# Attention scores as three float32r products of split keys and queries in a fused attention and two-layer MoE kernel

## The chip, the cores and the metric

The program runs on one NeuronCore of a Trainium2 chip. The metric is device time in microseconds (us) of one execution; lower is better. PE is TensorE, DVE is VectorE, ACT is ScalarE, POOL is GpSimd, SP is the engine whose queue issues the transfers.

## What is computed

Inputs are float32: attention with 2 batches, 8 heads, 576 positions and 64 values per head, with a bias on every score that comes out of a small network of the distance of two positions, and then two layers of the form activation(x @ w_in) @ w_out over 1152 tokens.

```python
scores = scale * np.matmul(q, k.transpose(0, 1, 3, 2))
x = (psi_rel / psi_i)[..., None]
bias = np.maximum(x @ w1 + b1, 0.0) @ w2
scores = scores + bias.transpose(2, 0, 1)[None]
attn = softmax(scores)                     # over the last axis
x = np.matmul(attn, v)                     # tokens x 512
h = x @ moe_w_in;   x = (max(h, 0) + alpha * min(h, 0)) @ moe_w_out
h = x @ moe2_w_in;  g = (a0 + a1 h + a2 h^2 + a3 h^3) / (1 + |b0| |h| + |b1| h^2 + 1e-6)
out = g @ moe2_w_out
```

## The kernel before

**Attention.** The queries are cut into nine blocks (BLOCKS): eight of 128 queries of one batch, and a last one with the 64 remaining queries of both batches side by side. Each block has four steps, one for a pair of heads, so there are 36 steps, 0 to 35; steps 32 to 35 are those of the last block. The two heads of a pair lie on partitions 0 to 63 and 64 to 127, of keys and of queries alike.

A step goes through these functions: `scores` (L326) multiplies keys and queries on PE, each head in its own half of the array's rows, 288 columns at a time, both operands float32, which the compiler makes two instructions of each; `row_max` (L338, DVE) adds the bias and takes the row's maximum; `expo` (L349, ACT) exponentiates and sums; `flip` (L361, L365, PE) transposes the result in nine pieces; `flip_out` (L371 and L375 on DVE, L377 on ACT) copies them out of PSUM; `values` (L389, PE) multiplies by the values. There is room in PSUM for the scores of one step only (pool `ps_s`), and the ninth transposed piece of step n goes into a spare corner of the scores of step n+1 where the new order holds, so PE can write scores of a step only after `row_max` has read those of the step before.

After a block's last step `inverse` (L400 to L402, DVE) takes 1/sum, `block_scale` (L442, DVE) applies it, and `block_split` (L450 on ACT, L451 on POOL) writes the result as a high part, rounded to float32r, and the low rest.

**Bias.** Between the steps the bias of the next blocks is made, in rows j, r: `hidden` (L228 on ACT, L230 on DVE), `bias_mm` (L244, PE), `bias_out` (L256 and L263 on ACT, L258 and L265 on DVE), and `bias_move`, a transfer on SP's queue (L270, L274). Row set j = 0 is made before step 0. For j = 4, the last block's 64 queries, the rows are made for partitions 0 to 63 and `bias_again` (L278) copies them to partitions 64 to 127 on DVE, in four pieces after steps 29 to 32.

**MoE.** Weights come in as 64-bit pieces; `unit_scale`, `unit_rest` (L613, L617, ACT) and `unit_join` (L621, L624, DVE) put a float32 together, `unit_high` (L644 on ACT, L646 on DVE) rounds it to float32r and `unit_low` (L651) subtracts for the rest. The first 12 units (`UHS`) have the rounding on DVE and the subtraction on POOL, the others have them on ACT and DVE. All MoE products are three float32r products, high by high, high by low and low by high (`up` L682, `down` L697).

**Order.** Nothing is reordered by the tools. Each call is put on an agenda with a planned time out of the table `Z`, and the agenda, sorted by that time, is the program order on every engine. `step_time(n)` is the planned start of step n. Two orders of a step exist: the older one, where flips and bias products alternate, and a new one for steps `FIRST` to `LAST`, 8 to 35, where the flips of step n-1 follow the scores of step n and the values are multiplied in four column tiles of 32 (`wide`) rather than two of 64.

Of the kernel before, what the change touches and what calls it, by code (L numbers as in the profile page):

```python
# [11 lines left out]
F32 = mybir.dt.float32  # L12
# [38 lines left out]
def row_tables():  # L51
# [54 lines left out]
def fused_kernel(ctx: ExitStack, tc: tile.TileContext, qT, q4T, kT, vp, m1_in, m1_out, m2_in, m2_out, small, ttab, out):  # L106
# [46 lines left out]
    xu_p = open_pool("xu", 1, "left")  # L153
    rq_p = open_pool("rq", 3, "left")
    bb_p = open_pool("bb", 1, "left")
# [19 lines left out]

    KT = [ac.tile([P, 4, S], F32, name=f"kt{b}") for b in range(B)]
    V = [ac.tile([P, 5, H, D], F32, name=f"v{b}") for b in range(B)]
# [17 lines left out]

    queries = {}

    def load_k(b, hp):
        nc.sync.dma_start(out=KT[b][:, hp], in_=kT[b, :, hp])

# [3 lines left out]
    def load_q(k):  # L204
        ib, b = BLOCKS[k]
        t = rq_p.tile([P, 4, P], F32, tag="rq", name="q")
        if ib < 4:
            nc.sync.dma_start(out=t, in_=qT[ib, b])
        else:
            for b in range(B):  # L210
                nc.sync.dma_start(out=t[:, :, 64 * b : 64 * b + 64], in_=q4T[b])
        queries[k] = t

    bias, hid, bev, bps = {}, {}, {}, {}
# [52 lines left out]
    def bias_move(j, r):  # L267
        be, bt = bev.pop((j, r)), bias[j]
        if j < 4:
            nc.sync.dma_start(out=bt[r::8].rearrange("p h j -> p (h j)"), in_=be)  # L270
        else:
            for i in range(2):
                rows = bt[2 * r + i : 64 : 8].rearrange("p h j -> p (h j)")
                nc.sync.dma_start(out=rows, in_=be[64 * i : 64 * i + 64])  # L274

    def bias_again(h):

        nc.vector.tensor_copy(out=bias[4][64:, h : h + 2], in_=bias[4][:64, h : h + 2])  # L278

# [29 lines left out]

    FIRST, LAST = 8, 36  # L310
    ptile, pps, tps, ptt, sums, pvs, spare = {}, {}, {}, {}, {}, {}, {}

    def scores(n):

        k, hp = divmod(n, 4)
        ib, b = BLOCKS[k]
        ptile[n] = p_p.tile([P, 2, S], F32, tag="p", name="p")
        if hp == 0:
            sums[k] = sm_p.tile([P, H], F32, tag="sums", name="sums")
        for u in range(2):  # L320
            pps[n, u] = ps_s.tile([P, 2, 512], F32, tag="s", name="s")
        for w in range(2):
            for bb, cols in [(b, slice(0, P))] if ib < 4 else [(0, slice(0, 64)), (1, slice(64, P))]:
                for u in range(2):
                    rows = slice(64 * u, 64 * u + 64)
                    nc.tensor.matmul(  # L326
                        out=pps[n, u][cols, w, :HALF], lhsT=queries[k][rows, hp, cols],
                        rhs=KT[bb][rows, hp, w * HALF : (w + 1) * HALF], start=True, stop=True,
                    )
        spare[n] = pps[n, 1][:, 1, HALF : HALF + P]  # L330
# [95 lines left out]
    def by_tensor(k):  # L426
        return k >= 6
# [60 lines left out]
    for n in range(NSTEP):  # L488
# [12 lines left out]
        if hp == 3:  # L501
            ag.at(t + Z["inv"], inverse, k)
            scale = t + 3 * DT + Z["new_bscale"] if FIRST <= n + 2 < LAST else t + 3 * DT + Z["bscale"]
            if by_tensor(k):
# [17 lines left out]
    NWA, NWC, NWB, NMID, NSP = 5, 2, 13, 13, 3  # L522
    UHS, USP = 12, 48
    NW = NWA + NWC + NWB
# [47 lines left out]
    def next_pools():  # L572
        for key in ("ba", "bb", "rq"):
            close_pool(key)
# [63 lines left out]
    def unit_high(j):  # L638
# [284 lines left out]
```

## Time and profile before

| | us |
|---|---|
| median of 3 runs | 604.25 (603.94 to 604.37) |
| profiled execution, its own time | 604.18 |
| its span | 602.4 |
| mean granted TensorE clock | 0.997 of full speed |
| PE busy | 586.9 (97%) |
| DVE busy | 500.1 (83%) |
| ACT busy | 427.4 (71%) |
| POOL busy | 41.7 (7%) |

The span is the time from the first to the last instruction; the execution has 1.8 us around it. Busy time is the time in which at least one instruction of the engine was under way. PE's instructions overlap one another, so their mean duration is longer than the pace at which they follow each other. Windows below are given in us from the span's start. The attention runs to about 188 us, and the MoE takes the rest.

### The profile page before, as it was taken

How to read it: one execution, taken by the hardware profiler on the slowest of the kernel's cores; microseconds unless marked ns; L12 is line 12 of the kernel's file. 1: busy time of each engine (PE TensorE's matmuls, PEld its weight loads, DVE VectorE, ACT ScalarE, POOL GpSimd, SP SyncE). 2: the span in 40 equal slices, each digit the busy share in tenths (PEclk: the TensorE clock that was granted, in tenths of full speed). 3: DMA queues.
4: the chain of work that ended last, by engine and by line, in shares of the span. 5: the costliest groups of instructions: out<-in, count | busy, mean ns of one | idle time of the engine just before them, and what ended most of it. 6: DMA issues, size and time to landing. Idle time of an engine off the chain costs nothing.

```text
span 602.4 us, 11747 instructions
## 1 busy us (share of the span) xinstructions
PE 586.9 (97%) x4678; PEld 504.3 (84%) x4678; DVE 500.1 (83%) x837; ACT 427.4 (71%) x716; POOL 41.7 (7%) x35
## 2 busy tenths in 40 slices
PE   8899999999989999999999999999999999999997
PEld 5356666666767999999999999998999999899985
DVE  6687788887698967779998779989999999779783
ACT  6678889888777656576675567797777887655660
POOL 0000000000022321000000302100000000000000
PEclk9899999999999999999999999999999999999999
DMA  5893323342723334344555477767000000001011
GB/s 169 263 231 107 92 73 103 81 104 62 187 72 100 112 106 139 114 154 156 172 149 174 131 207 217 215 203 262 19 2 1 0 1 0 2 2 52 1 52 54
DMA packets 41239, 65.31 MB, mean 108 GB/s; under 512 B 4016, under 2 KB 23776, under 8 KB 41184
## 3 DMA queue, kind: packets, MB, share of 16 engines
q1 hardware_dynamic: 41040, 64.21, 36.4%
q8 instruction: 37, 0.61, 0.4%
q10 hardware_dynamic: 144, 0.35, 0.2%
q14 instruction: 18, 0.15, 0.1%
HBM read 47.35 MB, written 6.58 MB: 90 GB/s over the span
## 4 chain that ended last, share of the span: by engine, by line
PE 83%; DVE 8%; ACT 4%; DMA 2%; issue 2%; SPq 0%; ACTq 0%; DVEq 0%
PE ops L697 30%; PE hps L682 30%; PE bps L244 6%; PE s L326 5%; PE pv L389 5%; PE tp L365 4%; DVE p L338 1%; DVE mid L621 1%; PE s L361 1%; ACT pt L377 1%; DVE mid L624 1%; DMA away<-mid 1%; DVE w L651 1%; ACT p L349 1%; DMA bias<-be 1%
## 5 line engine op out<-in xcount | busy, mean ns | idle before, releaser
L682 PE MATMUL hps<-xh,w 128*128 128x384 f32 x768 | 204.1, 336 | 0.0
L682 PEld LDWEIGHTS hps<-xh,w 128*128 128x128 f32 x768 | 139.6, 188 | 1.3 <-issue 0.2
L682 PE MATMUL hps<-xl,w 128*128 128x384 f32 x384 | 128.7, 335 | 0.0
L697 PE MATMUL ops<-g,w 128*128 128x384 f32 x576 | 104.5, 336 | 0.0
L697 PE MATMUL ops<-w,g 128*128 128x512 f32 x432 | 102.5, 392 | 1.2 <-DVE acc L769 1.2
L697 PEld LDWEIGHTS ops<-g,w 128*128 128x128 f32 x576 | 100.8, 188 | 0.0
L697 PEld LDWEIGHTS ops<-w,g 128*128 128x128 f32 x432 | 80.7, 188 | 17.6 <-issue 1.5
L349 ACT ACTIVATE p<-p,nm 128x576 f32<-128x576 f32 x72 | 55.7, 773 | 28.1 <-DVE nm L338 28.0
L682 PEld LDWEIGHTS hps<-xl,w 128*128 128x128 f32 x384 | 72.1, 188 | 0.9
L752 ACT CAST g<-n 128x768 fp32r<-128x768 f32 x48 | 40.1, 835 | 40.0 <-DVE n L716 28.3
L338 DVE CUSTOM_DVE_ANT_0 p<-s,bias 128x576 f32<-128x576 f32 x72 | 52.1, 753 | 14.1 <-PE s L326 8.9
L621 DVE SCALAR_TENSOR_TENSOR mid<-mid,raw 128x512 int32<-128x512 int32 x64 | 50.4, 787 | 12.5 <-ACT mid L613 12.4
L244 PE MATMUL bps<-h,w2s 128*32 128x288 f32 x576 | 51.4, 421 | 5.0 <-DVE be L258 2.5
L230 DVE TENSOR_SCALAR h<-tt,sc,nb 128x576 f32<-128x576 f32 x98 | 53.4, 582 | 0.0
L757 DVE TENSOR_TENSOR g<-n,g 128x768 fp32r<-128x768 f32 x48 | 46.5, 968 | 7.8 <-ACT g L752 7.8
L624 DVE SCALAR_TENSOR_TENSOR mid<-raw,mid 128x512 int32<-128x512 int32 x64 | 50.3, 786 | 2.2
L326 PE MATMUL s<-kt,q 64*128 64x288 f32 (+1 forms) x320 | 46.1, 433 | 1.4 <-DVE nm L338 0.8
L389 PE MATMUL pv<-pt,v 128*32 128x128 f32 (+2 forms) x1200 | 46.8, 267 | 0.0
L389 PEld LDWEIGHTS pv<-pt,v 128*32 128x32 f32 (+1 forms) x1200 | 40.4, 119 | 7.3 <-issue 2.7
L617 ACT ACTIVATE raw<-raw 128x512 int32<-128x512 uint32 x64 | 43.4, 678 | 2.7 <-DMA raw<-in_moe_w_in_dram 1.4
L613 ACT ACTIVATE mid<-raw 128x512 f32<-128x512 f32 x64 | 42.4, 662 | 0.0
L228 ACT ACTIVATE h<-tt,sm,sc 128x576 f32<-128x576 f32 x46 | 39.3, 863 | 3.0 <-DVE sc L172 2.5
(75 smaller groups left out, 734.4 us busy)
## 6 DMA issues: line engine op xcount, KB each, us to landing
raw<-in_moe_w_in_dram SPq DMA_DIRECT2D x32, 512.0 KB, 4.6
raw<-in_moe_w_out_dram SPq DMA_DIRECT2D x32, 512.0 KB, 3.7
bias<-be SPq DMA_DIRECT2D x32, 288.0 KB, 4.1
away<-mid SPq DMA_DIRECT2D x16, 256.0 KB, 4.9
mid<-away SPq DMA_DIRECT2D x16, 256.0 KB, 4.2
v<-in_vp_dram SPq DMA_DIRECT2D x10, 256.0 KB, 6.8
kt<-in_kT_dram SPq DMA_DIRECT2D x8, 288.0 KB, 5.7
out_dram<-acc SPq DMA_DIRECT2D x9, 256.0 KB, 2.1
```

Source lines behind the costliest of these rows:

```text
L230: nc.vector.tensor_scalar(out=h, in0=x, scalar1=sc[:, k : k + 1], scalar2=nb1, op0=ALU.mult, op1=ALU.max)
L244: nc.tensor.matmul(out=ps[32 * c : 32 * c + 32], lhsT=w2s, rhs=hid[j, r, c][:, u * HALF : (u + 1) * HALF], start=True, stop=True,)
L326: nc.tensor.matmul(out=pps[n, u][cols, w, :HALF], lhsT=queries[k][rows, hp, cols], rhs=KT[bb][rows, hp, w * HALF : (w + 1) * HALF], start= ...
L338: nc.vector.tensor_tensor_reduce(out=ptile[n][:, u, :].rearrange("p (w j) -> p w j", w=2), in0=pps.pop((n, u))[:, :, :HALF], in1=bias[j][: ...
L349: nc.scalar.activation(out=p, in_=p, func=AF.Exp, bias=nms.pop((n, u)), scale=-1.0, accum_out=sums[k][:, h : h + 1])
L389: nc.tensor.matmul(out=pv[64 * u + d : 64 * u + d + wide, hp, cols], lhsT=V[bb][:, j, 2 * hp + u, d : d + wide], rhs=pt[:, 4 * u + j if j ...
L617: nc.scalar.activation(out=low, in_=low.bitcast(U32), func=AF.Copy, scale=0.90625 * 2.0 ** -29, bias=0.24)
L621: nc.vector.scalar_tensor_tensor(out=m, in0=m, scalar=3, in1=raw[:, :, 0], op0=ALU.logical_shift_left, op1=ALU.bitwise_or)
L624: nc.vector.scalar_tensor_tensor(out=m, in0=raw[:, :, 1], scalar=-(2 ** 31), in1=m, op0=ALU.bitwise_and, op1=ALU.bitwise_or)
L682: nc.tensor.matmul(out=ps, lhsT=a, rhs=b, start=(i == 0), stop=(i == len(prs) - 1))
L697: nc.tensor.matmul(out=ops[ly, c, m], lhsT=a, rhs=b, start=(f == fs[0] and i == 0), stop=(f == fs[-1] and i == 2))
L757: nc.vector.tensor_tensor(out=gt[:, 1], in0=tmp.pop(p), in1=gt[:, 0].bitcast(F32), op=ALU.subtract)
```

## The change

1. **Scores.** Keys come into a raw tile (`kraw`) and are split once into `KH` (a cast to float32r, ACT, `cast_k`) and `KL` (the rest, DVE, `low_k`), one pair for each batch and head pair: eight casts, eight subtractions. The queries of a block are split in the same way by `split_q` into two parts, both on DVE. A score is now qh by KH, qh by KL and ql by KH, added up in PSUM: 12 float32r products of 288 columns in a step in place of 4 float32 ones. In the last block the queries of each batch are laid into a tile of full width with zeros (POOL) in the other batch's half, and both batches' products are added up: 24 products in a step.
2. **Order.** `FIRST` is 2 in place of 8: steps 2 to 7 go over to the new order with 32-wide values. `inverse` is planned 5.65 after the start of its step in place of 4.03, which is behind the next step's `row_max`, and `block_scale` moves from 3.3 to 5.8 for the blocks that spread the inverse by transfers.
3. **Bias of the last block.** `bias_again` is gone; its rows are sent twice by transfer, 16 transfers in place of 8.
4. **First 12 weight units.** `UHS` is gone: all roundings are on ACT and all subtractions on DVE.
5. The raw queries have one buffer in place of three; the split ones have three.

```diff
-    FIRST, LAST = 8, 36
+    FIRST, LAST = 2, 36
...
+    def cast_k(b, hp):
+        nc.scalar.copy(out=KH[b][:, hp], in_=kraw[b, hp])
+
+    def low_k(b, hp):
+        nc.vector.tensor_tensor(
+            out=KL[b][:, hp], in0=kraw.pop((b, hp)), in1=KH[b][:, hp].bitcast(F32), op=ALU.subtract
+        )
...
+    def split_q(k, part):
+        ib, b = BLOCKS[k]
+        for bb, o, e in [(b, 0, P)] if ib < 4 else [(0, 0, 64), (1, 64, P)]:
+            q = q_p.tile([P, 4, P], F32R, tag=f"q{part}", name="q")
+            if ib == 4:
+                nc.gpsimd.memset(q.bitcast(F32)[:, :, 64 - o : 128 - o], 0.0)
+            raw = queries[k][:, :, o:e]
+            if part == 0:
+                nc.vector.tensor_copy(out=q[:, :, o:e], in_=raw)
+            else:
+                high = qs[k, bb][0][:, :, o:e].bitcast(F32)
+                nc.vector.tensor_tensor(out=q[:, :, o:e], in0=raw, in1=high, op=ALU.subtract)
+            qs.setdefault((k, bb), []).append(q)
...
-            for bb, cols in [(b, slice(0, P))] if ib < 4 else [(0, slice(0, 64)), (1, slice(64, P))]:
+            for i, (q, kk) in enumerate(terms):
                 for u in range(2):
                     rows = slice(64 * u, 64 * u + 64)
                     nc.tensor.matmul(
-                        out=pps[n, u][cols, w, :HALF], lhsT=queries[k][rows, hp, cols],
-                        rhs=KT[bb][rows, hp, w * HALF : (w + 1) * HALF], start=True, stop=True,
+                        out=pps[n, u][:, w, :HALF], lhsT=q[rows, hp, :], rhs=kk[rows, hp, w * HALF : (w + 1) * HALF],
+                        start=(i == 0), stop=(i == len(terms) - 1),
                     )
...
-            for i in range(2):
-                rows = bt[2 * r + i : 64 : 8].rearrange("p h j -> p (h j)")
-                nc.sync.dma_start(out=rows, in_=be[64 * i : 64 * i + 64])
+            for o in (0, 64):
+                for i in range(2):
+                    rows = bt[o + 2 * r + i : o + 64 : 8].rearrange("p h j -> p (h j)")
+                    nc.sync.dma_start(out=rows, in_=be[64 * i : 64 * i + 64])
...
-            ag.at(t + Z["inv"], inverse, k)
-            scale = t + 3 * DT + Z["new_bscale"] if FIRST <= n + 2 < LAST else t + 3 * DT + Z["bscale"]
+            ag.at(t + (Z["new_inv"] if FIRST <= n + 1 < LAST else Z["inv"]), inverse, k)
+            scale = t + 3 * DT + Z["bscale"]
+            if FIRST <= n + 2 < LAST:
+                scale = t + 3 * DT + Z["new_iscale" if by_tensor(k) else "new_bscale"]
...
+            ag.at(step_time(4 * k - 2 + part) + Z["splitq"] if k else Z[f"splitq{part}"], split_q, k, part)
...
-        if j >= UHS:
-            nc.scalar.copy(out=out, in_=mids[j])
-        else:
-            nc.vector.tensor_copy(out=out, in_=mids[j])
+        nc.scalar.copy(out=out, in_=mids[j])
...
-        eng = nc.gpsimd if j < UHS else nc.vector
-        eng.tensor_tensor(out=w[:, 1, :], in0=mids.pop(j), in1=w[:, 0, :].bitcast(F32), op=ALU.subtract)
+        nc.vector.tensor_tensor(out=w[:, 1, :], in0=mids.pop(j), in1=w[:, 0, :].bitcast(F32), op=ALU.subtract)
...
-        ag.at(step_time(29 + h // 2) + Z["again"], bias_again, h)
```

What this makes of the order is seen at three places. In the rows below a line number is that of the kernel they come from; after the change the functions named above stand some 30 lines further down.

PE in steps 2 and 3 before (s are scores, tp transposed pieces, bps bias products, pv values; one row is a run of like instructions):

```order
L326 MATMUL s<-kt_131,q 128x288 x4
L244 MATMUL bps<-h,w2s 32x288 x4
L365 MATMUL tp<-ident,p 128x128 x4
L389 MATMUL pv<-pt,v_133 64x128 x10
L244 MATMUL bps<-h,w2s 32x288 x4
L365 MATMUL tp<-ident,p 128x128 x4
L361 MATMUL tp<-ident,p 128x128
L244 MATMUL bps<-h,w2s 32x288 x4
L326 MATMUL s<-kt_131,q 128x288 x4
```

and PE in steps 2 and 3 of the changed kernel:

```order
L355 MATMUL s<-kh_134,q 128x288 x2
L355 MATMUL s<-kl_136,q 128x288 x2
L355 MATMUL s<-kh_134,q 128x288 x4
L355 MATMUL s<-kl_136,q 128x288 x2
L355 MATMUL s<-kh_134,q 128x288 x2
L390 MATMUL s<-ident,p 128x128
L394 MATMUL tp<-ident,p 128x128 x8
L271 MATMUL bps<-h,w2s 32x288 x4
L418 MATMUL pv<-pt,v_138 32x128 x20
L271 MATMUL bps<-h,w2s 32x288 x8
```

The four score products of a step have become twelve, and the transposed pieces stand together behind them.

DVE from its last bias row of j = 0 to the first `row_max` (the row `p,nm<-s,bias`), as a run of 7 hidden rows, before:

```order
L230 TENSOR_SCALAR h<-tt,sc,nb_123 128x576 x7
L265 TENSOR_SCALAR be<-bps_310,cv 128x576
L230 TENSOR_SCALAR h<-tt,sc,nb_123 128x576 x2
L338 ISA p,nm<-s,bias 128x576
L338 ISA nm 128x1
```

and in the changed kernel:

```order
L257 TENSOR_SCALAR h<-tt,sc,nb_126 128x576 x7
L238 TENSOR_TENSOR q<-q 128x512
L292 TENSOR_SCALAR be<-bps_319,cv 128x576
L209 TENSOR_TENSOR kl_136<-kraw,kh_134 128x576 x2
L257 TENSOR_SCALAR h<-tt,sc,nb_126 128x576 x2
L367 ISA p,nm<-s,bias 128x576
L367 ISA nm 128x1
```

The second part of block 0's queries now stands ahead of the last `bias_out`, and so, some rows earlier among the hidden rows, does its first part; two key subtractions stand behind it.

DVE around step 32, from the `row_max` of step 31's first head on, before:

```order
L338 ISA p,nm<-s,bias 128x576
L338 ISA nm 128x1
L646 CAST w<-mid 128x512
L338 ISA p,nm<-s,bias 128x576
L338 ISA nm 128x1
L371 COPY pt<-s 128x128
L621 SCALAR_TENSOR_TENSOR mid<-mid,raw 128x512
L624 SCALAR_TENSOR_TENSOR mid<-raw,mid 128x512
L278 COPY bias<-bias 64x1152
L400 TENSOR_SCALAR rs<-sums 128x8
L401 RECIPROCAL rs<-rs 128x8
L402 TENSOR_SCALAR rs<-rs 128x8
```

and in the changed kernel:

```order
L367 ISA p,nm<-s,bias 128x576
L367 ISA nm 128x1
L367 ISA p,nm<-s,bias 128x576
L367 ISA nm 128x1
L400 COPY pt<-s 128x128
L657 SCALAR_TENSOR_TENSOR mid<-mid,raw 128x512
L660 SCALAR_TENSOR_TENSOR mid<-raw,mid 128x512
L238 TENSOR_TENSOR q<-q 128x4x64 x2
L367 ISA p,nm<-s,bias 128x576
L367 ISA nm 128x1
```

The copy of bias rows, the weight cast and the inverse no longer stand between the `row_max` of step 31 and that of step 32, and the second split of the last block's queries does.

## Rows read from the trace of the kernel before

**Rows 1.** The page, busy time, share of the span and instructions of each engine
```profile
PE 586.9 (97%) x4678; PEld 504.3 (84%) x4678; DVE 500.1 (83%) x837; ACT 427.4 (71%) x716; POOL 41.7 (7%) x35
```
**Rows 2.** Windows: us, busy us of each engine (instructions), PEclk, DMA share, GB/s
```profile
31.74:62.47 30.73, 30.73 (x329) 18.50 (x328) 23.83 (x62) 25.36 (x54) 1.28 (x1) 1.00 0.64 157
...
95.07:99.97 4.90, 4.71 (x77) 3.10 (x73) 4.02 (x9) 4.90 (x13) 1.30 (x1) 1.00 0.44 114
...
171.51:187.75 16.24, 12.58 (x173) 8.94 (x171) 13.62 (x30) 11.02 (x25) 4.21 (x3) 1.00 0.30 98
187.75:602.39 414.64, 409.16 (x2332) 388.57 (x2330) 354.92 (x470) 275.80 (x407) 27.50 (x19) 1.00 0.32 99
```
**Rows 3.** Timeline of PE, step 10: start us, us, engine line op xcount
```profile
71.72 1.24 PE L326 MATMUL s<-kt,q 64*128 64x288 f32 x8
72.89 0.33 PE L361 MATMUL s<-ident,p 128*128 128x128 f32 x1
...
76.32 0.51 PE L326 MATMUL s<-kt,q 64*128 64x288 f32 x2
```
**Rows 4.** Score instructions: the line's durations; timelines of PE and PEld inside step 10
```profile
L326 PE MATMUL s<-kt,q x320: 402/403/743, 20.8 to 188.6; 64*128 64x288 f32 x128, 64*64 64x288 f32 x32
...
72.07 0.65 PE L326 MATMUL s<-kt,q 64*128 64x288 f32 x4
...
72.31 0.19 PEld L326 LDWEIGHTS s<-kt,q 64*128 64x128 f32 x2
```
**Rows 5.** Timeline of PE, float32r products of 512 and 384 columns in the MoE
```profile
449.82 3.12 PE L697 MATMUL ops<-w,g 128*128 128x512 f32 x13
452.77 0.34 PE L682 MATMUL hps<-xh,w 128*128 128x384 f32 x1
...
454.51 0.33 PE L682 MATMUL hps<-xl,w 128*128 128x384 f32 x1
```
**Rows 6.** Timeline of DVE up to the first row_max (waits in brackets)
```profile
19.25 0.82 DVE L265 TENSOR_SCALAR be<-bps,cv 128x576 f32<-128x576 f32 x1
...
23.92 0.76 DVE L338 CUSTOM_DVE_ANT_0 p<-s,bias 128x576 f32<-128x576 f32 x1 [2.88 <-DMA kt<-in_kT_dram]
```
**Rows 7.** Groups by shape: busy us, mean ns of one | idle before
```profile
L651 DVE TENSOR_TENSOR w<-mid,w 128x512 fp32r<-128x512 f32 x52 | 35.5, 684 | 0.0
L644 ACT CAST w<-mid 128x512 fp32r<-128x512 f32 x52 | 31.9, 616 | 10.8 <-PE hps L682 10.8
L646 DVE CAST w<-mid 128x512 fp32r<-128x512 f32 x12 | 6.0, 496 | 0.0
```
**Rows 8.** Timelines of DVE and of PEld around step 20
```profile
119.00 0.16 DVE L400 TENSOR_SCALAR rs<-sums 128x8 f32<-128x8 f32 x1
...
119.52 0.17 DVE L788 TENSOR_SCALAR sm<-sm 128x16 f32<-128x16 f32 x1
...
122.81 0.16 PEld L244 LDWEIGHTS bps<-h,w2s 128*32 128x32 f32 x8 [0.56 <-ACT be L256]
```
**Rows 9.** DMA issues (us to landing, last); timelines of SP and ACT, first unit
```profile
raw<-in_moe_w_in_dram SPq DMA_DIRECT2D x32, 512.0 KB, 4.6
...
157.49 0.41 SPq L603 DMA_DIRECT2D raw<-in_moe_w_in_dram  x1
...
163.95 0.66 ACT L617 ACTIVATE raw<-raw 128x512 int32<-128x512 uint32 x1
```
**Rows 10.** Timelines of PE, POOL and DVE, steps 31 to 32
```profile
169.95 1.53 POOL L451 TENSOR_TENSOR xl<-xu,xh 128x512 fp32r<-128x512 f32 x1 [15.27 <-ACT xh L450]
171.44 1.73 POOL L651 TENSOR_TENSOR w<-mid,w 128x512 fp32r<-128x512 f32 x1
...
171.51 1.20 PE L326 MATMUL s<-kt,q 64*64 64x288 f32 x16
...
172.07 1.65 DVE L624 SCALAR_TENSOR_TENSOR mid<-raw,mid 128x512 int32<-128x512 int32 x1
173.75 0.75 DVE L278 COPY bias<-bias 64x1152 f32<-64x1152 f32 x1
```

More of the change, by code (lines that the diff above doesn't have):

```diff
@@ L153, in fused_kernel @@
     xu_p = open_pool("xu", 1, "left")
-    rq_p = open_pool("rq", 3, "left")
+    rq_p = open_pool("rq", 1, "left")
+    q_p = open_pool("q", 3, "left")
     bb_p = open_pool("bb", 1, "left")
@@ L174, in fused_kernel @@
     nc.vector.memset(cv, 0.0)
-    KT = [ac.tile([P, 4, S], F32, name=f"kt{b}") for b in range(B)]
+    KH, KL = ([ac.tile([P, 4, S], F32R, name=f"{x}{b}") for b in range(B)] for x in ("kh", "kl"))
     V = [ac.tile([P, 5, H, D], F32, name=f"v{b}") for b in range(B)]
@@ L194, in const_bias @@
         nc.vector.tensor_copy(out=cv[0:64, 1:2], in_=cps[0:64, 0:1])
-    queries = {}
+    kraw, queries, qs = {}, {}, {}
     def load_k(b, hp):
-        nc.sync.dma_start(out=KT[b][:, hp], in_=kT[b, :, hp])
+        tag = ["xh0", "xl0", "xh1", "xl1", "xh2", "xl2", "xh1", "xl1"][4 * b + hp]
+        kraw[b, hp] = xp.tile([P, S], F32, tag=tag, name="kraw")
+        nc.sync.dma_start(out=kraw[b, hp], in_=kT[b, :, hp])
+    def cast_k(b, hp):
[4 more added lines that the diff above has]
+        )
     def load_v(b, j):
@@ L271, in bias_move @@
         else:
-            for i in range(2):
-                rows = bt[2 * r + i : 64 : 8].rearrange("p h j -> p (h j)")
-                nc.sync.dma_start(out=rows, in_=be[64 * i : 64 * i + 64])
-    def bias_again(h):
-        nc.vector.tensor_copy(out=bias[4][64:, h : h + 2], in_=bias[4][:64, h : h + 2])
+            for o in (0, 64):
+                for i in range(2):
+                    rows = bt[o + 2 * r + i : o + 64 : 8].rearrange("p h j -> p (h j)")
+                    nc.sync.dma_start(out=rows, in_=be[64 * i : 64 * i + 64])
     def bias_rows_beside(j, r, at, step, at0, step0):
@@ L321, in scores @@
             pps[n, u] = ps_s.tile([P, 2, 512], F32, tag="s", name="s")
+        terms = []
+        for bb in [b] if ib < 4 else range(B):
+            qh, ql = qs[k, bb]
+            terms += [(qh, KH[bb]), (qh, KL[bb]), (ql, KH[bb])]
         for w in range(2):
-            for bb, cols in [(b, slice(0, P))] if ib < 4 else [(0, slice(0, 64)), (1, slice(64, P))]:
+            for i, (q, kk) in enumerate(terms):
                 for u in range(2):
@@ L466, in fused_kernel @@
             ag.at(Z[f"load_k{b}{hp}"], load_k, b, hp)
+            ag.at(Z[f"cast_k{b}{hp}"], cast_k, b, hp)
+            ag.at(Z[f"low_k{b}{hp}"], low_k, b, hp)
         for j in range(5):
@@ L515, in fused_kernel @@
     ag.at(0.05, load_q, 0)
+    for k in range(len(BLOCKS)):
+        for part in range(2):
+            ag.at(step_time(4 * k - 2 + part) + Z["splitq"] if k else Z[f"splitq{part}"], split_q, k, part)
     HB = 1.95
@@ L522, in fused_kernel @@
     NWA, NWC, NWB, NMID, NSP = 5, 2, 13, 13, 3
-    UHS, USP = 12, 48
+    USP = 48
     NW = NWA + NWC + NWB
@@ L572, in next_pools @@
     def next_pools():
-        for key in ("ba", "bb", "rq"):
+        for key in ("ba", "bb", "q", "rq"):
             close_pool(key)
@@ L793, in fused_kernel @@
     ag.at(step_time(20), moe_consts)
-    for h in range(0, H, 2):
-        ag.at(step_time(29 + h // 2) + Z["again"], bias_again, h)
     ag.at(EARLY, early_pools)
```

5 rows, old and new, of the table Z are left out of this document.

## Prediction

> **What bounds the kernel now.** I read the page first: PE is busy for 97% of the span, DVE for 83%, ACT for 71% [rows 1]. Such a share is a mean over stages, so the windows come next [rows 2]. From step 35 on, 187.75 us to the end, PE is busy for 409.16 of 414.64 us: that is the MoE, and the change touches nothing of its products. Whatever is gained must therefore be gained by bringing step 35 forward. In steps 2 to 7 (31.74 to 62.47) PE is busy all the time, DVE for 23.83 and ACT for 25.36 of 30.73. In steps 32 to 34 (171.51 to 187.75) no engine is full: PE has 12.58 of 16.24, DVE 13.62, ACT 11.02; there the steps hang on chains between engines. And there are single steps in which ACT is the full one: in step 15, 95.07 to 99.97, it is busy for 4.90 of 4.90. So PE bounds most of the attention, with ACT and DVE not far behind.
>
> The timeline of PE gives the length of a step in the new order, 76.32 - 71.72 = 4.60 us, of which the scores take 72.89 - 71.72 = 1.17 [rows 3]. They are eight instructions, two of each float32 product. Inside, four of them cover 0.65 us where one alone lasts 0.40 [rows 4]: so pairs of the two heads start together and the next pair follows 0.25 later. Four pairs are 0.97, and 0.20 is left for loading the first weights and for draining.
>
> All sums are made against the profiled execution, 604.18 us, which is 0.07 under the median of the runs; I forecast them as one.
>
> **Scores, steps 0 to 31.** No float32r product of 288 columns is in this trace. In the MoE, 13 of 512 columns take 452.77 - 449.82 = 2.95 us, 0.227 each, and ten of 384 columns take 454.51 - 452.77 = 1.74, 0.174 each [rows 5]. That is 0.053 for 128 columns, so 288 columns are 0.134 by the line through both. If they cost as much as 384 columns, they are 0.174, which is the upper bound; the lower is 0.053 x 288 / 128 = 0.12. I take 0.134, since the two rows differ in nothing but columns and 288 is not far from 384. If the two heads' products run side by side as they do in float32, a step has six pairs, 6 x 0.134 + 0.20 = 1.00 in place of 1.17: -0.17. Step 0 waits for its bias in any case. Steps 1 and 8 to 31 are 25 steps: -4.2. ACT gives part of that back: in steps like 15, two in eight (the two rows whose third hidden row is ACT's), it is full already [rows 2], so six of the 24 gain nothing: +1.0.
>
> **The start.** The first row_max starts at 23.92, 3.85 us after the last bias_out of row set 0 ends at 20.07, and DVE has waited 2.88 for that bias to land [rows 6]. That bias_out itself has no wait ahead of it: DVE is the engine that sets its time. The two query splits of block 0 stand ahead of this bias_out: a cast of 128x512, 0.50, and a subtraction, 0.68 [rows 7], less some overlap. That is +1.0, and nothing covers it. The two key subtractions that follow, 2 x 0.77 (0.68 x 576 / 512), fit into the wait of 2.88.
>
> **Steps 2 to 7.** The new order takes 4.60 where these six now take 30.73 / 6 = 5.12, and the scores another 0.17 less: on PE alone 6 x 0.69 = -4.1. But four key casts fall here on ACT, 4 x 0.69 (0.616 x 576 / 512), and on DVE four key subtractions, 4 x 0.77, and two blocks' query splits, 2 x 1.18 [rows 7]. ACT comes to 25.36 + 2.8 = 28.2 and DVE to 23.83 + 5.4 = 29.3. Back-to-back instructions overlap by about 0.08, so both can be run in some 27 to 28 us, but three engines that wait for each other will not all be full. Between 0 and -4.1 I take -1.5, which is what DVE's sum leaves.
>
> **inverse moved.** At 119.00 the three small instructions of inverse stand ahead of row_max and take 0.52, and later PE waits 0.56 for ACT, which runs late by that [rows 8]. The same stands ahead of the row_max that comes before steps 12 and 24. Behind row_max they delay nobody: three times up to 0.5, -1.4. Below nothing it can't go much, since block_scale, which waits for the inverse, moves back with it.
>
> **Steps 31 to 35.** On DVE a copy of bias rows goes from the chain, 0.75 at 173.75. The join at 172.07 takes 1.65 because POOL subtracts beside it, from 171.44 to 173.17 [rows 10]; an instruction of that shape with two inputs takes 0.68 by itself [rows 7]. With POOL's subtraction on DVE (0.68 too, in a place where DVE waits for ACT) that is another -1.0. Against it stand three things. The scores have twelve pairs, 12 x 0.134 + 0.20 = 1.8 in place of 1.2 [rows 10]; four times +0.6, of which the chain shows perhaps one, as PE is busy for 77% here. The weight cast on ACT, 0.62, comes between two expos, for perhaps +0.3. And step 32's scores wait for POOL to zero half a query tile, behind its subtraction, which runs from 169.95 to 171.48: about +0.7. In sum -0.1, between -2 and +2.5.
>
> **The rest.** The last bias rows cost eight more transfers on SP, ahead of the first weight unit. That unit is issued at 157.49, lands some 4.6 later, and ACT takes it at 163.95 [rows 9]: 1.9 us of cover, which two or three issues ahead of it use up nearly; beyond it each us goes to ACT. Twelve more weight casts on ACT and twelve subtractions on DVE lie mostly in the MoE, where PE is full and ACT has 275.80 of 414.64 [rows 2]: nothing. The raw queries' single buffer costs nothing: block k's second split is planned in step 4k - 1, and the load that overwrites its tile only after step 4k has begun.
>
> Sum: -4.2 + 1.0 + 1.0 - 1.5 - 1.4 - 0.1 = -5.2, that is **599.0 us**.
>
> **Rivals.**
> *PE alone decides.* If ACT and DVE keep up throughout, steps 2 to 7 give -4.1 and the give-back of 1.0 and the losses at the end go: -4.2 + 1.0 - 4.1 - 1.4 - 1.9 = -10.6, 593.6 us. For it: every one of the 30.73 us of steps 2 to 7 is PE's now. Against it: 29.3 us of DVE there.
> *ACT and DVE take the bound over.* Steps 2 to 7 stay at 5.1, and of the 24 later steps half keep their length: +1.0 - 2.1 - 0.7 - 0.1 = -1.9, 602.3 us; with a bad end 604.8. For it: step 15, where ACT is full already. Against it: most steps leave ACT and DVE 0.4 to 1.0 us.
> *The heads' products take turns.* If two float32r products in the two halves of the rows can't stream together, a step has 12 x 0.134 + 0.20 = 1.81, +0.64 over 32 steps, and the last block 24 x 0.134 + 0.20 = 3.4, +2.2 four times: 20.5 + 8.8, less some 3 for the rest, 630 us, slower. It decides from a pair pace of about 0.158 on: 220 pairs or so lie on the path, 0.22 us for each ns, and 5.2 us is 24 ns. Against it: float32 pairs do start together [rows 4]. No float32r pair is in the trace.
> *Weights wait for products.* A pair would take a load of 0.19 [rows 4] and then 0.134: 6 x 0.32 + 0.20 = 2.1, +0.95 in each of 32 steps, 30 us, and another 12 in the last block, 641 us. Against it: at 72.31 two loads run while products of the same rows are under way [rows 4], and the pair pace of 0.25 has no room for 0.19 more. The Trainium skill says in TensorE: Matmul & The Clock Gate, section Part 3: Packing small matmuls, that loading weights overlaps with matmuls under way only when their row groups differ. By that rule every pair here would load first, since it uses both row groups again; the trace disagrees for float32, so this has 1%.
>
> **How the numbers follow.** The forecast 0.55, PE alone 0.17, take-over 0.20, turns 0.07, weights 0.01. A measurement can tell from no change what is over 0.2%, 1.2 us. The forecast and PE alone are faster; of the take-over 0.12 is faster, 0.05 within, 0.03 slower; turns and weights are slower. So 0.84, 0.05, 0.11. PE alone is a floor, so the time of that case lies at 593.6 or a little above. The range runs from there to the take-over with a little more lost, 593.5 to 603.5, and leaves out turns, weights and the upper part of the take-over, together some 0.17.
>
> **What would show it.** Right: twelve score instructions of one step within 1.00 us and pairs 0.13 apart; steps 9 to 11 at 4.40; the first row_max near 24.9; step 35's scores near 182.5 us and the MoE from there as long as now. Wrong: pairs 0.27 apart; steps 2 to 7 still at 5.1 with ACT or DVE full; PE waiting at step 32 for POOL by more than 1 us; or PE idle in the MoE for more than the 5.5 us it is now.

## The result and the profile after

The changed kernel takes 612.64 us, median of 4 runs (611.95 to 613.72), beside 604.11 for the kernel before on the same chip: a ratio of 1.0142, interval 1.0125 to 1.0160. Forecast were 599.0 and, with 0.84, a faster kernel. It is slower, outside the range. The profiled execution took 611.95, its span 610.1.

The page's busy times of the changed kernel, which answer to [rows 1]:

```profile
PE 585.5 (96%) x4958; PEld 515.6 (85%) x4958; DVE 506.6 (83%) x861; ACT 438.2 (72%) x736; POOL 24.9 (4%) x27
```

PE is not busier than before, ACT by 11 us and DVE by 6. So the 7.7 us that the span grew are not PE's work, and the windows of the changed kernel, which answer to [rows 2], say where: steps 2 to 7, steps 8 to 29, step 30, steps 31 to 34, and from step 35 on (columns as there).

```profile
33.39:62.45 29.06, 27.88 (x472) 19.73 (x472) 26.99 (x68) 26.48 (x56) 0.09 (x1) 1.00 0.55 151
62.45:160.16 97.71, 96.64 (x1615) 70.78 (x1612) 83.42 (x223) 87.20 (x187) 8.29 (x8) 1.00 0.37 96
160.16:175.85 15.69, 6.07 (x59) 5.49 (x57) 3.44 (x9) 6.31 (x14) 0.00 (x0) 0.67 0.90 184
175.85:194.96 19.11, 17.20 (x239) 14.84 (x238) 14.16 (x35) 14.36 (x31) 1.78 (x3) 1.00 0.29 87
194.96:610.10 415.14, 409.76 (x2340) 389.70 (x2338) 353.42 (x472) 280.42 (x417) 14.01 (x10) 1.00 0.32 99
```

Step 30 alone takes 15.69 us, where it took 4.60 (163.36 to 167.96 before). Every engine is idle in most of it; only the DMA engines are nearly full, 0.90. The timelines of SP, ACT and PE of the changed kernel there, which answer to [rows 9] (L303 are the bias transfers, L639 the weight unit's load, L653 ACT's first instruction on it, L452 is `block_out`, L418 `values`):

```profile
149.77 7.71 SPq L303 DMA_DIRECT2D bias<-be  x11
158.13 0.40 SPq L639 DMA_DIRECT2D raw<-in_moe_w_in_dram  x1
159.30 2.25 SPq L223 DMA_DIRECT2D q<-in_q4T_dram  x2
...
170.24 0.65 ACT L653 ACTIVATE raw<-raw 128x512 int32<-128x512 uint32 x1 [9.38 <-DMA raw<-in_moe_w_in_dram]
170.80 0.64 ACT L649 ACTIVATE mid<-raw 128x512 f32<-128x512 f32 x1
171.34 0.57 ACT L452 COPY xu<-pv 128x512 f32<-128x512 f32 x1
...
161.31 1.04 PE L394 MATMUL tp<-ident,p 128*128 128x128 f32 x8
171.97 2.40 PE L418 MATMUL pv<-pt,v 128*64 128x128 f32 x20 [9.62 <-ACT xu L452]
```

The first unit is issued at 158.13, only 0.64 later than before (157.49). But ACT stands 9.38 us for it, and `block_out`, which empties the PSUM that PE's `values` need, stands behind it in ACT's order. The chain of the changed kernel (start, length, what) has the transfer in one piece:

```profile
158.13 12.09 DMA raw<-in_moe_w_in_dram
...
171.44 0.49 ACT xu L452
...
171.97 2.40 PE pv L418 x20
```

It lands 12.09 us after its issue; 4.6 is the median in [rows 9]. What it stands behind is seen in the windows' last two columns, the DMA engines' share and GB/s. In the changed kernel, a stretch in which nearly only last bias rows move:

```profile
152.00:158.00 6.00, 6.00 (x99) 4.90 (x92) 3.78 (x14) 5.50 (x14) 1.77 (x3) 1.00 0.53 120
```

and in the kernel before, the last bias rows there (152.00), bias rows of the other blocks (102.00) and weights (163.00):

```profile
152.00:155.00 3.00, 3.00 (x33) 1.94 (x29) 2.50 (x7) 1.94 (x5) 1.28 (x1) 1.00 0.54 128
102.00:103.20 1.20, 1.20 (x28) 0.81 (x29) 1.20 (x6) 1.15 (x4) 0.00 (x0) 1.00 0.85 221
163.00:165.30 2.30, 2.30 (x23) 1.65 (x20) 1.77 (x3) 2.30 (x6) 0.00 (x0) 1.00 1.04 342
```

A transfer of the last bias rows is 64 x 2304 bytes, 147 KB; at 120 GB/s that is 1.23 us, with the DMA engines busy by half. Sixteen are 19.7 us, and eleven of them are issued in the 7.71 us from 149.77 on, 0.70 each, faster than they drain. The transfers' packets in the trace show that it is not the whole unit that stands: 256 of its 512 pieces of 1024 bytes move from 159.26 to 162.46, beside the bias rows, and the next such piece moves at 164.50; the last piece of a bias row starts at 167.59.

What was predicted of the scores came as predicted. The timeline of PE of the changed kernel, step 10, which answers to [rows 3, 4]:

```profile
72.19 0.40 PE L355 MATMUL s<-kh,q 64*128 64x288 f32 x2
72.43 0.29 PE L355 MATMUL s<-kl,q 64*128 64x288 f32 x2
72.56 0.42 PE L355 MATMUL s<-kh,q 64*128 64x288 f32 x4
72.82 0.30 PE L355 MATMUL s<-kl,q 64*128 64x288 f32 x2
72.95 0.30 PE L355 MATMUL s<-kh,q 64*128 64x288 f32 x2
73.18 0.33 PE L390 MATMUL s<-ident,p 128*128 128x128 f32 x1
```

Pairs of the two heads start together, 0.13 apart, and what follows starts 0.99 after the first.

The spans side by side, with the run that has part 3 undone (first experiment below), from the starts of the steps in PE's timelines:

| stretch, us | before | changed | part 3 undone | forecast of the difference |
|---|---|---|---|---|
| start to step 1 | 26.47 | 28.02 | 28.29 | +1.0 |
| step 1 | 5.27 | 5.37 | 4.77 | -0.2 |
| steps 2 to 7 | 30.73 | 29.06 | 29.52 | -1.5 |
| steps 8 to 31 | 109.04 | 116.77 | 105.63 | -4.4 |
| steps 32 to 34 | 16.24 | 15.74 | 17.42 | -0.1 |
| step 35 and MoE | 414.64 | 415.14 | 414.97 | 0 |

### The profile page after: what moved, and what is told of

Read it like the earlier page. It is cut to its first block, busy times and chain, and to the rows that moved or that the text cites. A ratio compares the mean times of both kernels' runs of the same rounds, so it can differ in the third digit from the quotient of the medians.

```text
span 610.1 us, 12334 instructions
## 1 busy us (share of the span) xinstructions
PE 585.5 (96%) x4958; PEld 515.6 (85%) x4958; DVE 506.6 (83%) x861; ACT 438.2 (72%) x736; POOL 24.9 (4%) x27
## 4 chain that ended last, share of the span: by engine, by line
PE 76%; DVE 11%; ACT 5%; DMA 4%; issue 3%; SPq 0%; DVEq 0%; ACTq 0%
PE ops L729 29%; PE hps L714 29%; PE bps L271 5%; PE pv L418 4%; PE s L355 4%; PE tp L394 3%; DMA raw<-in_moe_w_in_dram 2%; DVE h L257 2%; DVE p L367 2%; DVE mid L657 1%; ACT pt L406 1%; DVE w L683 1%; ACT p L378 1%; PE s L390 1%; DMA away<-mid 1%
## 5 line engine op out<-in xcount | busy, mean ns | idle before, releaser
L657 DVE SCALAR_TENSOR_TENSOR mid<-mid,raw 128x512 int32<-128x512 int32 x64 | 47.2, 738 | 22.4 <-ACT mid L649 22.1
L418 PE MATMUL pv<-pt,v 128*32 128x128 f32 (+2 forms) x1320 | 47.7, 270 | 9.6 <-ACT xu L452 9.6
L418 PEld LDWEIGHTS pv<-pt,v 128*32 128x32 f32 (+1 forms) x1320 | 41.7, 117 | 17.3 <-ACT xu L452 9.9
L653 ACT ACTIVATE raw<-raw 128x512 int32<-128x512 uint32 x64 | 43.4, 677 | 11.3 <-DMA raw<-in_moe_w_in_dram 10.5
L660 DVE SCALAR_TENSOR_TENSOR mid<-raw,mid 128x512 int32<-128x512 int32 x64 | 47.4, 740 | 2.2
L679 ACT CAST w<-mid 128x512 fp32r<-128x512 f32 x64 | 39.3, 616 | 10.9 <-PE hps L714 10.9
L683 DVE TENSOR_TENSOR w<-mid,w 128x512 fp32r<-128x512 f32 x64 | 44.6, 698 | 0.0
```

Source lines behind the costliest of these rows:

```text
L418: nc.tensor.matmul(out=pv[64 * u + d : 64 * u + d + wide, hp, cols], lhsT=V[bb][:, j, 2 * hp + u, d : d + wide], rhs=pt[:, 4 * u + j if j ...
L653: nc.scalar.activation(out=low, in_=low.bitcast(U32), func=AF.Copy, scale=0.90625 * 2.0 ** -29, bias=0.24)
L657: nc.vector.scalar_tensor_tensor(out=m, in0=m, scalar=3, in1=raw[:, :, 0], op0=ALU.logical_shift_left, op1=ALU.bitwise_or)
L660: nc.vector.scalar_tensor_tensor(out=m, in0=raw[:, :, 1], scalar=-(2 ** 31), in1=m, op0=ALU.bitwise_and, op1=ALU.bitwise_or)
L683: nc.vector.tensor_tensor(out=w[:, 1, :], in0=mids.pop(j), in1=w[:, 0, :].bitcast(F32), op=ALU.subtract)
```

## The experiments

Theory A: the doubled bias transfers fill the DMA queue ahead of the first weight unit, and ACT's order hands the wait on. Theory B: the unit is late for another reason, the roundings on ACT or the last queries. Two more came up on the way: C, that it is the DMA engines' rate and not a queue's order, and D, that PE no longer bounds the attention.

**Part 3 undone** (`e1_again`).

```diff
-            for o in (0, 64):
-                for i in range(2):
-                    rows = bt[o + 2 * r + i : o + 64 : 8].rearrange("p h j -> p (h j)")
+            for i in range(2):
+                rows = bt[2 * r + i : 64 : 8].rearrange("p h j -> p (h j)")
...
+    for h in range(0, H, 2):
+        ag.at(step_time(29 + h // 2) + Z["again"], bias_again, h)
```

> The changed kernel with part 3 undone: 8 bias transfers for the last block and the copies on DVE. Theory A (the doubled bias transfers, 64 packets of 2304 B every 1.2 us, hold SP's queue until 167 and the first weight unit lands behind them, with ACT's block_out and PE's values queued behind the unit): step 30 goes from 15.7 us to about 4.4, the DVE copies take back 0.75, so 600 to 602 us, near the forecast of 599.0. Theory B (the unit is late for another reason: the roundings that now are all on ACT, or the last block's queries): step 30 stays over 12 us and the time stays near 612.

602.22 us, ratio 0.9967 (0.9955 to 0.9979): 10.4 less than the whole change. Its timelines of SP, ACT and PE:

```profile
154.60 0.42 SPq L642 DMA_DIRECT2D raw<-in_moe_w_in_dram  x1
...
160.73 0.19 ACT L381 ACTIVATION_READ_ACCUMULATOR p<-p,nm 128x1 f32 x1
160.82 0.66 ACT L656 ACTIVATE raw<-raw 128x512 int32<-128x512 uint32 x1
...
162.57 1.31 PE L421 MATMUL pv<-pt,v 128*64 128x128 f32 x20 [0.17 <-ACT xu L455]
163.82 1.09 PE L466 MATMUL tp<-ident,rs 128*64 128x128 f32 x16
...
170.28 0.53 PE L358 MATMUL s<-kh,q 64*128 64x288 f32 x4 [1.54 <-DVE q L238]
```

ACT no longer waits for the unit and step 30 is 4.62. A holds, though its range is missed by 0.2, and B falls. The wait is not only the landing's: ACT comes to the unit at 160.8 in both runs, but in the changed kernel the unit is issued 3.5 later (158.13 for 154.60), for SP has eight more to issue and its transfer L447 comes 2.5 later, behind the first of them, and then lands 12.09 after its issue, not 4.8. That is 10.8 us in all, of which 1.4 was to spare here. In step 32 a wait is left, 1.54 for the second query split. The stall also shows what the clock added: the values and the 16 pieces behind them take 2.27 us here (162.57 to 164.84), and 3.88 in the changed kernel (171.97 to 175.85), at the lower level of the clock (0.50 of full speed, 1.2 GHz), as the changed kernel's window of the values says (PEclk is the third from the end):

```profile
171.97:174.37 2.40, 2.40 (x22) 2.40 (x24) 1.29 (x4) 2.40 (x7) 0.00 (x0) 0.50 0.39 122
```

PE had stood for 9.62 us just before. So of the 11.1 us more in step 30, 9.5 are waiting and 1.6 the clock.

**Part 3 alone, on the kernel before** (`e2_double_alone`): the same lines the other way round.

> The kernel before with part 3 alone: 16 bias transfers, no copies on DVE. Theory A: the first unit lands 5 to 6 us later than at 163.9, ACT and then PE wait that long in step 30, 0.75 comes back from DVE: 608 to 611 us. Theory B: nothing but the copies changes, 603.4 us.

614.03 us, ratio 1.0162 (1.0147 to 1.0177). The direction is A's, the size above its range: ACT takes the unit at 172.78, 8.8 us later than in the kernel before and not 5 to 6, after a wait of 7.6:

```profile
172.78 0.65 ACT L614 ACTIVATE raw<-raw 128x512 int32<-128x512 uint32 x1 [7.55 <-DMA raw<-in_moe_w_in_dram]
```

There is the clock again, 0.50 for the values. So this one edit makes more than the whole loss, whatever the rest does.

**The first three units' loads on ACT's queue** (`e3_act_queue`).

```diff
+        issue = (nc.scalar if j < 3 else nc.sync).dma_start
...
-            nc.sync.dma_start(out=raw.rearrange("p (k f) w -> p k (f w)", k=4), in_=src)
+            issue(out=raw.rearrange("p (k f) w -> p k (f w)", k=4), in_=src)
```

> The changed kernel with the loads of the first three weight units issued on ACT's queue, all else as it is. If what holds the unit is the order in SP's queue (theory A), it lands 5 to 8 us after its issue, ACT goes on, and what is late next is the last block's queries, still behind the bias rows in SP's queue: 603 to 608 us. If what holds it is the rate of the DMA engines themselves, shared by all queues (theory C), it lands as late as now, near 170, and the time stays at 611 to 613.

612.71 us, as the change itself. The chain of this run:

```profile
152.90 9.08 DMA raw<-in_moe_w_in_dram
...
162.23 5.73 DMA raw<-in_moe_w_in_dram
...
169.97 6.11 DMA q<-in_q4T_dram
...
176.11 0.04 DVE q L235
```

Neither theory had this whole. The unit lands near 162, not 170, and ACT goes on: against C, though the unit is also issued 5.2 us earlier here. It takes 9.08 us, beside bias rows. What was late next was named right and its price, 603 to 608, wrong, for the edit brought a wait that neither theory has. The waits of SP in this run:

```profile
SPq L303 <- DMA raw<-in_moe_w_in_dram: 11.9, 3, 8.5
```

No bias row needs a weight; but in the trace the bias row that SP issues at 161.99, after 8.5 us, waits for the semaphore (the counter that tells of a landing) that the unit's load signals, since the transfers of both queues take turns with the same few. So the last two bias rows leave SP at 167.97 and 168.61, right behind the third unit's landing, the last block's queries land behind them at 176.1, and DVE waits 11.0 for these. The run as it is doesn't separate the order in a queue from the rate of the engines. The Trainium skill says in DMA: Bandwidth & Descriptors, section Rules for kernel authors, that spreading transfers over issuing engines doesn't add bandwidth, because all use the same 16 DMA engines. This run agrees: while weights of ACT's queue and bias rows of SP's move, the last column of its window is 174 GB/s, where step 30 of the changed kernel has 184:

```profile
153.50:162.00 8.50, 8.50 (x102) 7.14 (x99) 5.15 (x17) 6.03 (x15) 1.78 (x3) 1.00 0.85 174
```

**Doubling by two large transfers** (`e4_again_dma`), behind the third unit.

```diff
+        nc.sync.dma_start(out=bias[4][64:, h : h + 4], in_=bias[4][:64, h : h + 4])
```

> The changed kernel with 8 bias transfers and the doubling by two transfers of 64 partitions and 9 KB each inside the chip, behind the third weight unit in SP's queue. Theory A: no stall in step 30, no copies on DVE: 599 to 601 us, up to 1 less than with the copies on DVE. Theory B: near 612.

601.71 us, ratio 0.9957 (0.9940 to 0.9973). The same bytes, to 64 partitions in pieces of 9216 bytes and behind the units, cost nothing that shows: A, again a little above its range. Which of the two, the shape or the place, does it wasn't tried apart.

**Four of the eight second transfers** (`e9_dose`).

```diff
+            for o in (0, 64)[: 2 if r < 2 else 1]:
```

> The run with 8 bias transfers and DVE copies (602.2 us) with 4 of the 8 second transfers put back (those of the first two bias rows of the last block), copies kept: 12 transfers. Theory A (each transfer holds SP's queue for about 1.2 us, whatever the number): the first unit lands 4.9 us later than in that run, of which 1 to 2 are covered: 605 to 607 us. Theory F (the queue breaks down only at the full number, at a limit on what is outstanding): 602 to 603.

606.91 us, ratio 1.0047 (1.0029 to 1.0065): 4.7 more than without them, and the whole change with eight is 10.4 more. The timeline of ACT of this run has the wait:

```profile
163.66 0.69 ACT L657 ACTIVATE raw<-raw 128x512 int32<-128x512 uint32 x1 [3.36 <-DMA raw<-in_moe_w_in_dram]
```

The unit lands 4.2 later than with none of the eight (163.6 for 159.4), 1.05 for each, and with all eight 10.8 later, 1.35 for each. It grows by the transfer, with no threshold at the full number: A, against F. In the time the wait isn't alone: the values and the 16 pieces take 4.04 us (165.42 to 169.46) where they took 2.27, at the lower clock again.

With the cause settled, 602.2 is still 3.2 above the forecast. The other runs ask for that.

**Without the order part** (`e5_no_order`, on the run with part 3 undone) and **the order part alone** (`e6_order_alone`, on the kernel before). The first has

```diff
-    FIRST, LAST = 2, 36
+    FIRST, LAST = 8, 36
...
-            ag.at(t + (Z["new_inv"] if FIRST <= n + 1 < LAST else Z["inv"]), inverse, k)
+            ag.at(t + Z["inv"], inverse, k)
```

and the old plan of `block_scale`, and it puts `bo_scalar0`, the planned time of a `bias_out` on ACT, back from 2.35 to 2.9, which the change had moved too; the second has these the other way round.

> The run with 8 bias transfers and DVE copies (602.2 us) with part 2 undone as well: steps 2 to 7 in the older order, the inverse and its scaling where they were. Theory A (PE bounds these steps, and DVE's room decides what of it is kept): steps 2 to 7 take about 5.0 each in place of 4.9 and block edges give back some of the 1.4 put down to the inverse: 603 to 605.5 us. Theory D (the new order only fills engines that were full anyway and costs as much as it gives): 601.5 to 602.5.

> The kernel before with part 2 alone: new order and 32-wide values from step 2, the inverse and its scaling later; float32 scores, no splits, no other change. Theory A: without the casts and subtractions DVE (23.8 of 27.6) and ACT (25.4) have room in steps 2 to 7, so these come down from 5.12 to about 4.65 each, and the inverse gives up to 1.4: 599.5 to 602 us, as fast as the whole change without its transfers or faster. Theory D: 603.5 to 604.5.

602.86 us (ratio 0.9986, 0.9976 to 0.9997) and 601.67 (0.9960, 0.9947 to 0.9972). Alone, the order gives 2.4: steps 2 to 7 take 29.10 for 30.73, steps 8 to 31 108.06 for 109.04, by the starts of the steps. The rest of the change without part 3 and without the order gives 1.3. The two together should give 3.7 and give 1.9 (604.1 to 602.2): the order part is worth only 0.6, hardly more than can be told, where the scores are split already. For e6 A holds; for e5 A's range was missed by a little, D's too. The starts of the steps say where the gain goes. With the order alone, steps 12, 20 and 24, those that `inverse` held up, become shorter by 0.18, 0.34 and 1.00, but steps 8 and 16 longer by 0.40 and 0.35, and step 1 by 0.66. The cast of `block_split` on ACT stood in step 15 before and stands in step 16 with the new order, so ACT takes part of the gain there; the next run shows it.

**High by high alone** (`e7_high_only`, on the run with the large transfers): two of three products of a score left out.

```diff
-            terms += [(qh, KH[bb]), (qh, KL[bb]), (ql, KH[bb])]
+            terms += [(qh, KH[bb])]
```

> The run with the doubling by two large transfers (601.7 us) without two of the three products of a score: qh by KH alone is left, 4 products in a step and 8 in one of the last block; qh by KL and ql by KH are left out of the computation, the splits still run. Theory A (PE bounds most of the attention, ACT and DVE 0.2 to 0.7 behind it): 0.53 less of PE in a step, of which most steps keep 0.2 to 0.5: 588 to 594 us. Theory D (ACT and DVE have already taken the bound over): 597 to 601.

597.53 us, ratio 0.9890: 4.2 less than with all products, though the scores fall by 0.53 in each of 32 steps and by 1.06 in each of the last four, 21 in all. D: step 10 takes 4.27 in place of 4.42, in which PE was busy all the time. The timelines of PE and DVE in step 10 of this run:

```profile
71.83 0.53 PE L358 MATMUL s<-kh,q 64*128 64x288 f32 x4
72.29 0.33 PE L393 MATMUL s<-ident,p 128*128 128x128 f32 x1
...
71.97 0.52 DVE L285 TENSOR_SCALAR be<-bps,cv 128x288 f32<-128x288 f32 x1 [0.86 <-PE bps L271]
72.40 0.57 DVE L257 TENSOR_SCALAR h<-tt,sc,nb 128x576 f32<-128x576 f32 x1
72.89 0.75 DVE L370 CUSTOM_DVE_ANT_0 p<-s,bias 128x576 f32<-128x576 f32 x1
```

The scores are there at 72.36, but `row_max` starts at 72.89: a `bias_out` that waited for PE and a hidden row stand ahead of it in DVE's order. No engine is full there, as the first of the windows below says; by these rows the order of three engines is what bounds. In step 16 it is ACT. Its windows here, in the changed kernel and before:

```profile
71.83:76.10 4.27, 4.20 (x73) 2.69 (x70) 3.88 (x10) 4.14 (x11) 0.00 (x0) 1.00 0.61 156
...
98.20:103.31 5.11, 4.42 (x74) 2.77 (x70) 3.78 (x13) 5.11 (x12) 1.27 (x1) 1.00 0.43 112
99.30:104.40 5.10, 4.96 (x82) 3.31 (x78) 4.16 (x14) 5.10 (x12) 1.28 (x1) 1.00 0.42 112
99.97:104.73 4.76, 4.76 (x79) 3.19 (x75) 3.66 (x12) 4.71 (x11) 0.00 (x0) 1.00 0.25 65
```

ACT (the fourth of the engines' columns) is busy for all of step 16 after the change, with one instruction more, and the step keeps its length when PE loses 0.53. The 4.2 may be a little less than the products are worth by themselves, for step 34 of this run is 1.5 longer, 7.68 for 6.16, PE standing 2.0 for ACT and then working at the lower clock.

**Query splits moved** (`e8_splits`, on the run with the large transfers).

```diff
-    "splitq": 2.4, "splitq0": 9.3, "splitq1": 17.5,
+    "splitq": 2.4, "splitq0": 18.83, "splitq1": 18.84,
...
-            ag.at(step_time(4 * k - 2 + part) + Z["splitq"] if k else Z[f"splitq{part}"], split_q, k, part)
+            ag.at(step_time(4 * k - 2 + part * (k < 8)) + Z["splitq"] if k else Z[f"splitq{part}"], split_q, k, part)
```

> The run with the doubling by two large transfers (601.7 us) with both query splits of block 0 behind the last bias_out of row set 0 on DVE, and the second split of the last block right behind its first, a step earlier. Theory A (the splits ahead of the last bias_out delay the first row_max by 1.0, and step 32's scores stand 1.6 us for the second split): 599 to 600.2 us. Theory E (the first bias lands when the transfers let it, whatever DVE does, and step 32 then waits for its bias instead): 601 to 602.

599.33 us, ratio 0.9926 (0.9909 to 0.9942): 2.4 less; A holds, E falls. Step 1 starts at 26.65, not 27.91, and step 32 takes 4.16, not 5.96. The profiled execution is the fastest of six, 598.13, and PE keeps its full clock in it between 26 and 32, where the changed kernel and the run it stands on have 0.50; so the profile shows more of a gain than the medians do. DVE at the start of this run, beside the same of the changed kernel in the fence after it:

```profile
19.02 0.82 DVE L292 TENSOR_SCALAR be<-bps,cv 128x576 f32<-128x576 f32 x1
19.76 0.42 DVE L235 CAST q<-q 128x512 fp32r<-128x512 f32 x1
...
24.10 0.76 DVE L370 CUSTOM_DVE_ANT_0 p<-s,bias 128x576 f32<-128x576 f32 x1 [0.88 <-DMA kraw<-in_kT_dram]
```

```profile
19.85 0.81 DVE L292 TENSOR_SCALAR be<-bps,cv 128x576 f32<-128x576 f32 x1
...
24.97 0.76 DVE L367 CUSTOM_DVE_ANT_0 p<-s,bias 128x576 f32<-128x576 f32 x1 [1.99 <-DMA kraw<-in_kT_dram]
```

**Three tries on top of that** (each on `e8_splits`): part 4 undone (`e10_uhs`), three copies from ACT to DVE (`e11_flip`), six key subtractions on POOL (`e12_low_pool`).

```diff
+        eng = nc.gpsimd if j < 12 else nc.vector
```

```diff
-    "first_hidden_scalar_2", "first_hidden_scalar_6", "flip_vector_28", "flip_vector_32",
+    "first_hidden_scalar_2", "first_hidden_scalar_6", "flip_vector_7", "flip_vector_15", "flip_vector_23", "flip_vector_28", "flip_vector_32",
```

```diff
+        eng = nc.vector if (b, hp) < (0, 2) else nc.gpsimd
```

> The fastest run so far (doubling by two large transfers, query splits moved: 599.3 us) with part 4 undone: the first 12 units rounded on DVE and subtracted on POOL. Theory A (as predicted, POOL's subtractions slow DVE's joins in steps 31 to 35 by about 1.0, the cast on ACT costs 0.3 of it): 599.5 to 600.5 us. Theory G (ACT or DVE were short there, POOL was the better place): 598 to 599.

> The fastest run so far (599.3 us) with the second copy of transposed pieces of steps 7, 15 and 23 on DVE in place of ACT, 0.47 us of ACT in each of steps 8, 16 and 24. Theory D (ACT, full for 5.1 to 5.3 us in these steps, bounds them): 0.2 to 0.4 less in each: 598.2 to 598.8 us. Theory A (PE with its 4.97 to 5.02 bounds them): nothing, 599 to 599.6.

> The fastest run so far (599.3 us) with six of the eight key subtractions (all but the first two) on POOL in place of DVE. Theory D (DVE, busy 5.9 of 6.6 and 4.86 of 4.92, bounds steps 2 and 4): 1 to 2 us less: 597.3 to 598.5. Theory H (POOL takes twice as long for one and slows what DVE runs beside it, as at 167.8 in the run with DVE copies, where a join took 1.31 in place of 0.69): no gain or a loss, 599 to 601.

599.06, 599.26 and 599.03 us, ratios 0.9915 (0.9902 to 0.9929), 0.9919 (0.9906 to 0.9933) and 0.9920 (0.9905 to 0.9936): none can be told from 599.33. Part 4 is worth nothing either way, and for e10 neither range can be told from the other. For e12 H holds. The windows of steps 16 and 17 of e8,

```profile
97.28:102.39 5.11, 4.97 (x84) 3.32 (x80) 4.18 (x14) 5.11 (x12) 1.29 (x1) 1.00 0.42 112
102.39:106.77 4.38, 4.38 (x80) 3.28 (x79) 3.72 (x10) 3.53 (x9) 0.00 (x0) 1.00 0.15 44
```

and of e11,

```profile
98.67:103.77 5.10, 4.95 (x82) 3.30 (x79) 4.77 (x15) 5.10 (x12) 1.29 (x1) 1.00 0.41 112
103.77:108.14 4.37, 4.37 (x78) 3.24 (x77) 3.72 (x10) 3.05 (x8) 0.00 (x0) 1.00 0.14 42
```

show why the time is A's without A's reason: DVE has the copy more in step 16, but ACT has it less only in step 17, where it had room and PE is full. In step 16 ACT stays full with its 12 instructions, so D's claim on that step wasn't put to the test. In e12 step 4 falls from 4.93 to 4.64 and step 2 rises from 6.63 to 6.91.

## Why the prediction was wrong

- **The last bias rows: the step that failed.** "1.9 us of cover, which two or three issues ahead of it use up nearly" priced eight more transfers by the time that SP takes to issue them, and took the landing as 4.6 whatever stood in the queue; in the sum they were 0. The price is the drain: 1.23 us for each by the windows, and the unit lands 1.05 later for each of four and 1.35 for each of eight. Eight of them cost 10.4 us in time, the lower clock included, which no term had. "beyond it each us goes to ACT" was right. The rows for the price were there: eight such transfers are in the trace of before, and while they move it has 128 GB/s at a share of 0.54 (152.00 above). The Trainium skill has the reason in DMA: Bandwidth & Descriptors, section Why a DMA increments its semaphore by 16 and not by 1: a copy is split over as many engines, up to 16, as divide the outermost dimensions of both sides. The last bias rows go to 8 partitions at a time, the others to 16; the shares of 0.53 and 0.85 agree with 8 engines and 16, and so does the half of the unit that moved beside the bias rows.
- **Scores: right on PE.** Pairs 0.13 apart, 1.0 a step; steps 9 to 11 at 4.40, 4.42 and 4.42 where 4.40 was named. Heads' products taking turns, and weights that wait for products, are ruled out by the same rows.
- **Steps 2 to 7: the number is right**, -1.7 for -1.5 in the changed kernel, -1.2 with part 3 undone, in part by luck: it was what DVE's sum of 29.3 us left, and DVE is busy for 26.99 of 29.06, ACT for 26.48 where 28.2 was named. Step 2 grew from 5.63 to 6.35 and the other five gave 2.4. **The inverse: right** for the steps it named: -1.4 forecast, and with the order alone steps 12, 20 and 24 give 1.5.
- **Steps 8 to 31: too large a gain**, -3.4 (part 3 undone) for -4.4. Seventeen of the 24 steps give 0.12 to 0.19, which is what was forecast for the scores, and step 15, which was to give nothing, gives 0.47. What is missing stands at the edges of blocks: step 8 grows by 0.63 and step 16 by 0.36, in which ACT is nearly or wholly full (5.23 of 5.35 and 5.10 of 5.10 in the changed kernel), and of the steps of `inverse` only step 24 gives what it gave alone. The give-back put down to ACT was thus the right engine, but in other steps. The rival in which ACT and DVE take the bound over has 602.3, next to the 602.2 of the run with part 3 undone, but by luck: it had steps 2 to 7 stay at 5.1, where they take 4.9, and half of the later steps keep their length.
- **The start: right, but short.** The first `row_max` starts at 24.97 in the changed kernel, 24.9 was named. Of the 1.05 by which that is later than before, the last `bias_out` makes 0.60 (19.85 for 19.25), not 1.0; the rest is in the wait behind it. [rows 6] name a key transfer as what ended that wait; that it is the bias was inferred. Step 1 however starts 1.55 later, not 1.0. PE's clock is at 0.50 from 25.4 to 32.3 in the changed kernel, and before from 26.6 to 30.0; what that costs wasn't measured.
- **Steps 31 to 35: a wait not seen.** Named was POOL's zeroing. What step 32 stands for is the second split on DVE, 0.76 in the changed kernel and 1.54 with part 3 undone, behind two joins of a weight unit. The order showed it there, and the prediction read only what had left. Part 4, for which it had -1.0 of POOL and +0.3 of the cast, is worth nothing measurable on the run with the splits moved.
- **MoE:** a little longer from step 35 on: 414.97 us with part 3 undone, 415.44 with the splits moved, for 414.64. Why wasn't tried.

## What to carry to other kernels

Price an added transfer by how long it holds the DMA engines, not by its issue: bytes over the rate that transfers of the same shape show in the trace, and look up how many partitions its outermost dimension has. Then ask what is queued behind it, on which engine's order its consumer stands, and what else is behind that consumer. A stage in which one engine is busy all the time gives back only what the next chain leaves: here a cut of 0.53 us of PE in a step brought 0.15, and nothing in step 16, where ACT was full.

## What the runs showed that was not expected

- Transfers to 8 partitions move at 120 GB/s with the DMA engines at a share of 0.53, where those to 16 partitions have 221 at 0.85 and weights 342 at 1.04. Whether the last rows can be laid out for 16 engines wasn't tried.
- Another queue passes a full one by only in part: issued on ACT's queue the same unit took 9.08 us to land, with bias rows of SP's queue beside it, where behind them it took 12.09 and the run with part 3 undone shows a landing of 4.8. And SP then stood 8.5 us for that landing, so the time stayed.
- Two thirds of the products of all scores, 21 us of PE's time, are worth 4.2 us here.
- The best versions here take 599.0 to 599.3 us, the forecast time but not by the forecast's terms: they have two moves that the change lacks, the doubling in large transfers behind the first units, and the query splits where DVE has room.
